# A Fourier mixing and GELU feed-forward kernel: the order of ScalarE's work in a step, the place of one activation, and the steps that carry output sums and transforms

## The chip, the cores and the metric

The kernel runs on one core of one Trainium2 chip. The metric is the time of one execution on the device in microseconds (us). TensorE is PE in the profile (its weight loads are PEld), VectorE DVE, ScalarE ACT, GpSimd POOL, SyncE SP; SP only issues DMAs here. A measurement of this kernel repeats to about 0.2%.

## The reference

The input x is 8 sequences of 3008 rows of 256 numbers, float32. The first block takes a Fourier transform over the rows and then over the columns and keeps the real part; the second is a feed-forward layer with a GELU in its sigmoid form.

```python
X = np.fft.fft(x, axis=1)
X = np.fft.fft(X, axis=2)
x = X.real.astype(np.float32).reshape(8 * 3008, 256)
h = x @ w_in                                # 256 -> 2048
g = h * (1.0 / (1.0 + np.exp(-1.702 * h)))
out = (g @ w_out).astype(np.float32)        # 2048 -> 256
```

## The kernel before, in words

**Symmetry.** The input is real, so the real part of row k of the two transforms and that of its mirror row are a sum and a difference of the same two parts. The kernel transforms the rows only (`mix1`, `stage2`), folds the column transform into w_in once (`fold_w`), and makes for a block of 256 row numbers two products, P (cosine part) and Q (sine part). P + Q is what row k needs before the GELU, P - Q what the mirror row needs.

**Steps.** The work is a list of 384 steps (line 507): 8 sequences, 3 blocks, 2 halves of 256 (or 226) row numbers, and NP = 8 steps of 256 of the 2048 hidden features. A group is the eight steps of one half; outputs add up in PSUM over a group. The first 8 steps run in another form (`hidden`, `rows`). From step 8 on one step t does this:

- `middle(t)` (line 583): ACT writes a bias into the PSUM bank `x` of the step, two L590, one of two banks in turn (`b0`, `b1`).
- `begin(t)` (line 593): PE adds P to it, four matmuls of 128x64 weights and 256 columns (eight records in the trace). `doubled(t)` (line 599): ACT copies 2P to an SBUF tile g, L602. `begin(t, 1)`: PE adds Q, so that the bank holds P + Q. It must wait for L602.
- `forward(t)` (line 604): ACT applies the GELU to the bank and writes A11 and A12 (L605). `backward(t)` (line 607): VectorE takes 2P - (P + Q) with rows reversed (L563) and so has the argument of the mirror rows, in SBUF. `activate_back(t)` (line 611): ACT applies the GELU to it, A21 (L616) and A22 (L617).
- `sums(t)` (line 621): VectorE makes S3 and S1 (L624, L625), POOL S2 and S4 (L626, L627). `deeper` (line 640) does the like a level further down for a pair of steps: two L648 on VectorE a step.
- With a lag of three steps (`LAG`) PE multiplies by w_out, in two nested levels of a scheme with seven products for a 2x2 block matrix: `product` for the first of the seven (planned at 436 ns) and `small_product` for the others (222 ns a pair). Their list for a step comes from `units`, which joins what step t - 3 gives (`now`) and what the pair before left (`late`). The list is worked off in order by `issue(least)`, which issues while the planned cost stays within `least`.

The order of each engine's instructions is that of the program text; nothing reorders it.

**Order of a normal step, before** (line 1075 on): `begin(t, 1)`, `forward(t)`, `issue(1100)`, `begin(t + 1)`, the rest of the list, `backward(t)`, `activate_back(t)`, `doubled(t + 1)`, one `deeper`, `sums(t)`, `middle(t + 2)`, the output sums of `combine_small`, the other `deeper`. In a normal step A21 goes back into the bank `x` in PSUM (`there` is True); the bank is free for the bias of step t + 2 only after the sums.

**Special steps.** 50 steps carry a transform group: `mix1` (28 times; stage one of the next sequence, from input rows that POOL has folded in `fold1`) or `stage2` (22 times, with a small rotation and four transposes on VectorE, L351 and L370). Both borrow the banks `b0` and `b1`. In a special step the list of the next step is issued too, and A21 stays in SBUF (L616 writes `big`).

**End of a group.** Counted by t modulo 8 of the running step: in step 3 `combine` copies from PSUM by ACT (L776, L778, L779) and `combine_small` adds four times on VectorE (L808); `swap` moves halves between partitions by ACT (L817) in 4, 5 and 5; `combine_last` adds in step 6 (L826 twice, L790) and step 0 (L829); `turn_last` transposes in 1 and 2 (L759) and SP stores (L848).

Of the kernel before, what the change touches and what calls it, by code (L numbers as in the profile page):

```python
# [29 lines left out]
ALU = mybir.AluOpType  # L30
# [82 lines left out]
def kernel(ctx: ExitStack, tc, x, w_in, w_out, tab1, tab2, out):  # L113
# [497 lines left out]
    def activate_back(t, there):  # L611

        n = width(t)
        x = xb.pop(t)
        a21[t] = x[:, 0:n] if there else turned_rows(t, n)
        nc.scalar.activation(a21[t], turned_rows(t, n), ACTF.Gelu_apprx_sigmoid)  # L616
        nc.scalar.activation(right(t, A22, n), right(t, A22, n), ACTF.Gelu_apprx_sigmoid)  # L617

    a21 = {}

    def sums(t):

        n, a = width(t), a21.pop(t)
        nc.vector.tensor_tensor(right(t, S3, n), left(t, n), a, op=ALU.subtract)  # L624
        nc.vector.tensor_tensor(right(t, S1, n), a, right(t, A22, n), op=ALU.add)  # L625
        nc.gpsimd.tensor_tensor(right(t, S2, n), right(t, S1, n), left(t, n), op=ALU.subtract)  # L626
        nc.gpsimd.tensor_tensor(right(t, S4, n), right(t, A12, n), right(t, S2, n), op=ALU.subtract)  # L627
# [164 lines left out]
    def group_end(t):  # L792
        return t >= 0 and deep(t) and steps[t][3] == NP - 1

    def combine_small(t):
# [8 lines left out]
        for out, i0, i1 in ((res(RES, KEPT - RES), res(KEPT + 384, 0), both(2, [384, 2], [1, w])),  # L804
                            (res(KEPT + 128, 128), res(KEPT, 0), both(5, [384, 2], [1, w])),
                            (res(RES + 256 + w), res(KEPT + 256), both(5, [1, w])),
                            (res(RES + 256, w - 256), res(KEPT + 128, 128), both(3, [384, 2], [1, w]))):
            nc.vector.tensor_tensor(out, i0, i1, op=ALU.add)  # L808

    def swap(t, part):  # L810
# [8 lines left out]
    def combine_last(t, part):  # L819

        if not group_end(t):
            return
        n = width(t)
        if part == 0:
            for q in range(2):
                nc.vector.tensor_tensor(oc[:, q + 1, :n], oc[:, q, :n], big[:, RES + 1024 + 256 * q:RES + 1024 + 256 * q + n], op=ALU.add)  # L826
            fifth(free(big[:], RES + 768, [0, 2], [1, n]), n)
        else:
            nc.vector.tensor_tensor(oc[:, 0:3, :n], oc[:, 0:3, :n], free(big[:], RES, [256, 3], [1, n]), op=ALU.add)  # L829
# [154 lines left out]
    for b in range(1, B):  # L984
        t0 = (b - 1) * NBLK * NF
        if b == 1:
            loads, groups = (3, 3, 17, 24), (15, 22, 25, 32)
# [29 lines left out]
    n = len(steps)  # L1017
    pending = []

    def issue(least=None):  # L1020
        spent = 0
        while pending and (least is None or spent + pending[0][0] / 2 <= least):
            cost, fn, *args = pending.pop(0)
            fn(*args)
            spent += cost

    def transform(t):
        fn, args = special[t]
        spare[:] = [f"b{(t + 1) % 2}", f"b{t % 2}"]
        fn(*args)  # L1030
        middle(t + 1)
        while waiting:
            m, ps = waiting.pop()
            mixed(m, 1, ps)

    for t in range(n + LAG + 1):
        if t < NP:
# [36 lines left out]
        else:  # L1074
# [16 lines left out]
            if now:  # L1091
# [81 lines left out]
```

## Time and profile before

| what | us |
|---|---|
| median of 3 runs | 2050.18 |
| lowest and highest run | 2048.13 and 2052.48 |
| the profiled execution | 2047.31 |
| its span, first to last instruction | 2045.3 |
| from the start of L605 in step 24 to that in step 376 (44 groups) | 1817.7 |
| PE busy, PEld busy | 1869.8, 1464.5 |
| DVE, ACT, POOL busy | 1678.5, 1247.1, 1039.2 |

The granted TensorE clock is 0.998 over the span. The profile lists instructions by the line of the kernel's text; a tile name stands for all its buffers, and most of the work lies in one large SBUF tile `big`. In the table of waits a row reads: who waited, for whom, total us, times, longest. In the groups: count, busy us, mean ns of one, idle time of the engine just before them. In the timeline: start, us, engine, line, with the idle time before in brackets. Instructions of one engine overlap by some 0.08 us at their ends, so costs by starts are a little below the durations. Matmul ends are modelled.

### The profile page before, as it was taken

Reading aid. Unit: us, or ns where it says so; the run is one execution under the profiler, and the core shown is the slowest. Engines: PE = TensorE matmul, PEld = TensorE weight load, DVE = VectorE, ACT = ScalarE, POOL = GpSimd, SP = SyncE. Lnnn points to the kernel's source line nnn. Section 1 sums busy time; section 2 is a strip of 40 time slices with the busy share of each in tenths; the row PEclk is TensorE's granted clock in tenths of the full one; section 3 lists DMA queues with packets and bytes.
Section 4 is the critical chain, followed back from the end, with each engine's and each line's share of the span. In section 5 each row is a group of like instructions: output and inputs, shape, how many; then the busy total and the mean of one; then the engine's idle time right before and its main releaser. Section 6 shows DMA issues by size and latency. Waiting matters only on the chain. (4 is left out here: it accounts for less than half of the span.)

```text
span 2045.3 us, 61513 instructions
## 1 busy us (share of the span) xinstructions
PE 1869.8 (91%) x25990; PEld 1464.5 (72%) x25990; DVE 1678.5 (82%) x2629; ACT 1247.1 (61%) x2663; POOL 1039.2 (51%) x1053
## 2 busy tenths in 40 slices
PE   8988899999999999899998999999989999999998
PEld 5566767777677777777777777777767777777776
DVE  7978888888787888878788888888887888788885
ACT  6556556665666556566566666666656566656664
POOL 4756654445555555455554555554545544344342
PEclk9999999999999999999999999999999999999999
DMA  8322211212212122211222013210232012101001
GB/s 292 102 70 56 56 50 35 65 31 55 50 44 57 31 55 61 64 26 31 59 72 55 20 32 69 69 48 20 48 72 50 18 24 50 28 12 28 16 12 32
DMA packets 152407, 105.67 MB, mean 52 GB/s; under 512 B 108733, under 2 KB 133341, under 8 KB 151572
## 3 DMA queue, kind: packets, MB, share of 16 engines
q1 hardware_dynamic: 149300, 99.69, 20.0%
q8 instruction: 205, 3.36, 0.7%
q10 hardware_dynamic: 2832, 2.05, 0.4%
q14 instruction: 70, 0.57, 0.1%
HBM read 64.41 MB, written 48.05 MB: 55 GB/s over the span
## 5 line engine op out<-in xcount | busy, mean ns | idle before, releaser
L626 POOL TENSOR_TENSOR big<-big 128x256 f32<-128x256 f32 (+1 forms) x376 | 457.1, 1216 | 924.4 <-DVE big L625 924.3
L185 PE MATMUL x<-pq,wcs 128*64 128x256 f32 (+1 forms) x6016 | 773.8, 381 | 135.4 <-ACT g L602 126.1
L648 DVE TENSOR_TENSOR big<-big 128x768 f32<-128x768 f32 (+1 forms) x736 | 730.9, 993 | 0.0
L185 PEld LDWEIGHTS x<-pq,wcs 128*64 128x64 f32 x6016 | 388.4, 137 | 322.5 <-ACT g L602 166.0
L563 DVE TENSOR_TENSOR big<-g,x 128x512 f32<-128x512 f32 (+2 forms) x440 | 257.2, 596 | 327.6 <-ACT big L605 324.7
L590 ACT ACTIVATE x<-nb,af 128x256 f32<-128x256 f32 (+1 forms) x752 | 356.0, 473 | 165.0 <-DVE big L625 111.3
L685 PE MATMUL low<-big 128*64 128x128 f32 (+1 forms) x6624 | 425.7, 271 | 3.2 <-DVE big L808 2.9
L685 PEld LDWEIGHTS low<-big 128*64 128x64 f32 x6624 | 372.5, 137 | 47.5 <-issue 10.5
L616 ACT ACTIVATE x<-big 128x256 f32<-128x256 f32 (+1 forms) x326 | 124.9, 383 | 330.3 <-DVE big L563 326.4
L627 POOL TENSOR_TENSOR big<-big 128x256 f32<-128x256 f32 (+1 forms) x376 | 301.0, 801 | 29.5
L605 ACT ACTIVATE big<-x 128x512 f32<-128x512 f32 (+1 forms) x376 | 220.2, 586 | 109.3 <-PE x L185 64.6
L602 ACT ACTIVATE g<-x 128x512 f32<-128x512 f32 (+1 forms) x376 | 216.1, 575 | 64.2 <-PE x L185 64.0
L185 PE MATMUL top<-big,wo 128*64 128x256 f32 (+1 forms) x1536 | 227.3, 376 | 3.2 <-DVE os L759 3.2
L685 PE MATMUL mid<-big,wo 128*64 128x128 f32 (+1 forms) x2944 | 214.6, 271 | 0.0
L685 PEld LDWEIGHTS mid<-big,wo 128*64 128x64 f32 x2944 | 175.0, 137 | 21.9 <-DVE big L808 1.4
L685 PE MATMUL low<-big,wo 128*64 128x128 f32 (+1 forms) x2208 | 158.8, 272 | 4.5 <-DVE big L648 4.5
L685 PE MATMUL mid<-big 128*64 128x128 f32 (+1 forms) x2208 | 155.2, 270 | 0.0
L617 ACT ACTIVATE big<-big 128x256 f32<-128x256 f32 (+1 forms) x376 | 149.3, 397 | 0.0
L685 PEld LDWEIGHTS mid<-big 128*64 128x64 f32 x2208 | 130.6, 137 | 16.5
L685 PEld LDWEIGHTS low<-big,wo 128*64 128x64 f32 x2208 | 126.6, 137 | 18.8 <-DVE big L648 7.8
L185 PEld LDWEIGHTS top<-big,wo 128*64 128x64 f32 x1536 | 107.8, 137 | 42.2 <-DVE os L759 3.6
L624 DVE TENSOR_TENSOR big<-big,x 128x256 f32<-128x256 f32 (+1 forms) x326 | 132.4, 406 | 3.9 <-ACT x L616 3.9
(103 smaller groups left out, 1782.9 us busy)
## 6 DMA issues: line engine op xcount, KB each, us to landing
out_dram<-os SPq DMA_DIRECT2D x284, 64.0 KB
t<-Td SPq DMA_DIRECT2D x24, 512.0 KB
Td<-big SPq DMA_DIRECT2D x56, 192.0 KB
big<-in_x_dram SPq DMA_DIRECT2D x56, 128.0 KB
big<-Xr SPq DMA_DIRECT2D x56, 128.0 KB
nb<-Nd SPq DMA_DIRECT2D x23, 256.0 KB
out_dram<-os SPq DMA_DIRECT2D x96, 56.0 KB
Xr<-in_x_dram SPq DMA_DIRECT2D x7, 752.0 KB
```

The costliest lines, as they stand in the source:

```text
L185: nc.tensor.matmul(out[c0:c0 + 64], lhsT=lhs[:, c0:c0 + 64], rhs=rhs, skip_group_check=True, **how)
L563: nc.vector.tensor_tensor(free(out, at + m - 1, [by, 2], [RUN, blocks], [-1, m]), *ins, op=op)
L590: nc.scalar.activation(x[:, i * 256:i * 256 + n], nbt[b, blk][:, hh * 256:hh * 256 + n], ACTF.Copy, scale=af1[:, f:f + 1])
L602: nc.scalar.activation(two(g[:], n), two(xb[t][:], n), ACTF.Copy, scale=2.0)
L605: nc.scalar.activation(front(t), two(xb[t][:], width(t)), ACTF.Gelu_apprx_sigmoid)
L616: nc.scalar.activation(a21[t], turned_rows(t, n), ACTF.Gelu_apprx_sigmoid)
L617: nc.scalar.activation(right(t, A22, n), right(t, A22, n), ACTF.Gelu_apprx_sigmoid)
L624: nc.vector.tensor_tensor(right(t, S3, n), left(t, n), a, op=ALU.subtract)
L626: nc.gpsimd.tensor_tensor(right(t, S2, n), right(t, S1, n), left(t, n), op=ALU.subtract)
L627: nc.gpsimd.tensor_tensor(right(t, S4, n), right(t, A12, n), right(t, S2, n), op=ALU.subtract)
L648: nc.vector.tensor_tensor(out, i0, i1, op=how)
L685: nc.tensor.matmul(pot[name][64 * side:64 * side + 64, at:at + w], lhsT=lhs, rhs=rhs, start=first_in, stop=(p == NP - 2), skip_group_check ...
```

## The change

In a normal step the doubled copy of the next step follows `begin(t + 1)`, ahead of `backward` and `activate_back`, and only 436 ns of the list, not 1100, are issued ahead of `begin(t + 1)`. A21 stays in SBUF always; `middle(t + 2)` comes right after `activate_back`; both `deeper` parts come ahead of `sums`. `combine_small` does two of its four adds in step 3 and two in step 4; `combine_last` and the swaps come a step later, and the former is in three parts. Small products of two of the seven places (7 and 4) move from the list of step 1 of a group to that of step 2, and the first product of step 2 to the list of step 1. The transform groups move to steps with t modulo 8 of 2 and 6 (but for some of the first sequences), with changed amounts issued around them; the step ahead of a special one keeps 666 ns of its list for it. Loads and folds follow.

```diff
-        reversed_sum(big[:, at:at + 256], at_right(t, A22) - at, gt.pop(t), xb[t], width(t), ALU.subtract)
+        reversed_sum(big[:, at:at + 256], at_right(t, A22) - at, gt.pop(t), xb.pop(t), width(t), ALU.subtract)
...
-        x = xb.pop(t)
-        a21[t] = x[:, 0:n] if there else turned_rows(t, n)
-        nc.scalar.activation(a21[t], turned_rows(t, n), ACTF.Gelu_apprx_sigmoid)
+        nc.scalar.activation(turned_rows(t, n), turned_rows(t, n), ACTF.Gelu_apprx_sigmoid)
...
-        n, a = width(t), a21.pop(t)
+        n, a = width(t), turned_rows(t, width(t))
...
-        todo += [(436, product, t, *it) for it in plan(t)]
+        if p != 2 or not deep(t):
+            todo += [(436, product, t, *it) for it in plan(t)]
+        if p == 1 and deep(t):
+            now = [(436, product, t + 1, *it) for it in plan(t + 1)]
         if t >= NP and p % 2 and deep(t):
-            now = [(222, small_product, t, k, pr) for k in (1, 2, 4, 7) for pr in range(PAIRS)]
+            now = [(222, small_product, t, k, pr) for k in ((1, 2) if p == 1 else (1, 2, 4, 7)) for pr in range(PAIRS)] + now
         if t > NP and p % 2 == 0 and deep(t - 1):
-            late = [(222, small_product, t - 1, k, pr) for k in ((5, 6, 3) if p else (5, 3, 6)) for pr in range(PAIRS)]
+            late = [(222, small_product, t - 1, k, pr) for k in ((7, 4) if p == 2 else ()) + (5, 6, 3) for pr in range(PAIRS)]
...
-            loads, groups = (t0 - 21, t0 - 13, t0 - 4, t0 + 3), (t0 - 7, t0, t0 + 16, t0 + 32)
-            folds = [t0 + k for k in (-18, -15, -13, -10, -8, -6, -4, -2, 2, 5, 8, 11, 14, 18, 22, 26)]
+            loads, groups = (t0 - 21, t0 - 13, t0 - 4, t0 + 4), (t0 - 6, t0 + 2, t0 + 18, t0 + 26)
+            folds = [t0 + k for k in (-18, -15, -13, -10, -8, -6, -4, -2, 1, 4, 7, 10, 13, 16, 19, 22)]
...
-        for blk, k in enumerate((39, 56, 72)):
+        for blk, k in enumerate((38, 54, 70)):
...
-    def issue(least=None):
+    def issue(least=None, keep=0):
         spent = 0
+        if keep:
+            least = sum(u[0] for u in pending) - keep
...
             m, ps = waiting.pop()
             mixed(m, 1, ps)
+        middle(t + 2)
...
-            swap(t - LAG - 3, 1)
+            swap(t - LAG - 4, 2)
             combine(t - LAG - 1)
...
-                activate_back(t, False)
-                issue(1350)
+                activate_back(t)
+                issue(2000)
                 deeper(t - 2, 0)
                 deeper(t - 3, 2)
+                deeper(t - 2, 1)
+                deeper(t - 3, 3)
                 sums(t)
                 transform(t)
-                deeper(t - 2, 1)
-                deeper(t - 3, 3)
...
-                middle(t + 2)
-                issue(880)
+                issue(1000)
             else:
-                issue(0 if after else 1100)
+                issue(0 if after else 436)
                 if t + 1 < n:
                     begin(t + 1)
+                    doubled(t + 1)
+                swap(t - LAG - 3, 0)
...
-                issue()
-                if after and t + 1 < n:
-                    doubled(t + 1)
+                issue(keep=666 if soon else 0)
                 if t < n:
                     backward(t)
-                    activate_back(t, True)
-                if not after and t + 1 < n:
-                    doubled(t + 1)
+                if t - LAG - 1 != last:
+                    combine_small(t - LAG - 2, 1)
+                if t < n:
+                    activate_back(t)
+                if t + 2 < n and not soon:
+                    middle(t + 2)
                 deeper(t - 2, 0)
                 deeper(t - 3, 2)
+                deeper(t - 2, 1)
+                deeper(t - 3, 3)
                 if t < n:
                     sums(t)
-                if t + 2 < n and not soon:
-                    middle(t + 2)
-                combine_small(t - LAG - 1)
-                pending += held
-                issue()
-                deeper(t - 2, 1)
-                deeper(t - 3, 3)
-            swap(t - LAG - 2, 0)
-            swap(t - LAG - 3, 2)
-            combine_last(t - LAG - 4, 0)
-            combine_last(t - LAG - 6, 1)
+                combine_small(t - LAG - 1, 0)
...
+            swap(t - LAG - 3, 1)
+            combine_last(t - LAG - 5, 0)
+            combine_last(t - LAG - 5, 1)
+            combine_last(t - LAG - 6, 2)
```

More of the change, by code (lines that the diff above doesn't have):

```diff
@@ L608, in backward, with activate_back @@
         at = TMP + t % 2 * 256
-        reversed_sum(big[:, at:at + 256], at_right(t, A22) - at, gt.pop(t), xb[t], width(t), ALU.subtract)
-    def activate_back(t, there):
+        reversed_sum(big[:, at:at + 256], at_right(t, A22) - at, gt.pop(t), xb.pop(t), width(t), ALU.subtract)
+    def activate_back(t):
         n = width(t)
-        x = xb.pop(t)
-        a21[t] = x[:, 0:n] if there else turned_rows(t, n)
-        nc.scalar.activation(a21[t], turned_rows(t, n), ACTF.Gelu_apprx_sigmoid)
+        nc.scalar.activation(turned_rows(t, n), turned_rows(t, n), ACTF.Gelu_apprx_sigmoid)
         nc.scalar.activation(right(t, A22, n), right(t, A22, n), ACTF.Gelu_apprx_sigmoid)
-    a21 = {}
     def sums(t):
-        n, a = width(t), a21.pop(t)
+        n, a = width(t), turned_rows(t, width(t))
         nc.vector.tensor_tensor(right(t, S3, n), left(t, n), a, op=ALU.subtract)
@@ L793, in group_end, with combine_small @@
         return t >= 0 and deep(t) and steps[t][3] == NP - 1
-    def combine_small(t):
+    def combine_small(t, half):
         if not group_end(t):
@@ L806, in combine_small @@
                             (res(RES + 256 + w), res(KEPT + 256), both(5, [1, w])),
-                            (res(RES + 256, w - 256), res(KEPT + 128, 128), both(3, [384, 2], [1, w]))):
+                            (res(RES + 256, w - 256), res(KEPT + 128, 128), both(3, [384, 2], [1, w])))[2 * half:2 * half + 2]:
             nc.vector.tensor_tensor(out, i0, i1, op=ALU.add)
@@ L826, in combine_last @@
                 nc.vector.tensor_tensor(oc[:, q + 1, :n], oc[:, q, :n], big[:, RES + 1024 + 256 * q:RES + 1024 + 256 * q + n], op=ALU.add)
+        elif part == 1:
             fifth(free(big[:], RES + 768, [0, 2], [1, n]), n)
@@ L986 @@
         if b == 1:
-            loads, groups = (3, 3, 17, 24), (15, 22, 25, 32)
+            loads, groups = (3, 3, 17, 24), (15, 22, 26, 32)
             folds = 11, 12, 13, 14, 16, 17, 19, 20, 21, 22, 23, 24, 26, 28, 29, 30
         else:
-            loads, groups = (t0 - 21, t0 - 13, t0 - 4, t0 + 3), (t0 - 7, t0, t0 + 16, t0 + 32)
-            folds = [t0 + k for k in (-18, -15, -13, -10, -8, -6, -4, -2, 2, 5, 8, 11, 14, 18, 22, 26)]
+            loads, groups = (t0 - 21, t0 - 13, t0 - 4, t0 + 4), (t0 - 6, t0 + 2, t0 + 18, t0 + 26)
+            folds = [t0 + k for k in (-18, -15, -13, -10, -8, -6, -4, -2, 1, 4, 7, 10, 13, 16, 19, 22)]
         for k in range(3):
@@ L1108 @@
                 doubled(t + 1)
[L1109 to L1110 removed]
+                issue(1000)
             else:
[L1112 removed]
+                issue(0 if after else 436)
                 if t + 1 < n:
                     begin(t + 1)
+                    doubled(t + 1)
+                swap(t - LAG - 3, 0)
                 held = [pending.pop() for _ in range(5)][::-1] if t - LAG == last else []
[L1116 to L1118 removed]
+                issue(keep=666 if soon else 0)
                 if t < n:
                     backward(t)
[L1121 to L1123 removed]
+                if t - LAG - 1 != last:
[4 more added lines that the diff above has]
+                    middle(t + 2)
                 deeper(t - 2, 0)
                 deeper(t - 3, 2)
+                deeper(t - 2, 1)
+                deeper(t - 3, 3)
                 if t < n:
                     sums(t)
[L1128 to L1138 removed]
+                combine_small(t - LAG - 1, 0)
+                if held:
+                    combine_small(t - LAG - 1, 1)
+                    pending += held
+                    issue()
+            swap(t - LAG - 3, 1)
+            combine_last(t - LAG - 5, 0)
+            combine_last(t - LAG - 5, 1)
+            combine_last(t - LAG - 6, 2)
             turn_last(t - LAG - 7, 0)
```

## The prediction

> **What bounds the kernel now.** Names first: a step is one round of the loop over t; eight steps make a group, numbered here 0 to 7 by t modulo 8. I read the page's busy times first, then the table of waits over all engines.
>
> ```profile
> PE 1869.8 (91%) x25990; PEld 1464.5 (72%) x25990; DVE 1678.5 (82%) x2629; ACT 1247.1 (61%) x2663; POOL 1039.2 (51%) x1053
> ```
>
> ```profile
> POOL big L626 <- DVE big L625: 924.3, 348, 7.3
> ACT x L616 <- DVE big L563: 326.4, 190, 5.6
> DVE big L563 <- ACT big L605: 324.7, 211, 4.9
> PEld x L185 <- ACT g L602: 166.0, 162, 3.6
> PE x L185 <- ACT g L602: 126.1, 132, 3.2
> ACT x L590 <- DVE big L625: 111.3, 259, 1.4
> ...
> PEld x L185 <- ACT x L590: 39.3, 121, 0.8
> ```
>
> PE is the fullest engine, so only what it waits for counts: the doubled copy (L602), 166.0 us seen at the weight loads, 126.1 us at the matmuls, whose modelled ends cover part of each wait. The timeline of one step 4 shows why the copy is late.
>
> ```profile
> 984.98 0.60 ACT L605 ACTIVATE big<-x 128x512 f32<-128x512 f32 x1
> ...
> 985.79 1.03 PE L185 MATMUL x<-pq,wcs 128*64 128x256 f32 x8
> ...
> 986.65 0.83 PE L685 MATMUL mid<-big,wo 128*64 128x128 f32 x12
> ...
> 987.31 1.48 PE L685 MATMUL low<-big 128*64 128x128 f32 x24
> 987.94 0.68 DVE L563 TENSOR_TENSOR big<-g,x 128x512 f32<-128x512 f32 x1
> 988.54 0.95 DVE L648 TENSOR_TENSOR big<-big 128x768 f32<-128x768 f32 x1
> 988.65 0.39 ACT L616 ACTIVATE x<-big 128x256 f32<-128x256 f32 x1 [3.08 <-DVE big L563]
> 988.98 0.40 ACT L617 ACTIVATE big<-big 128x256 f32<-128x256 f32 x1
> 989.28 0.58 ACT L602 ACTIVATE g<-x 128x512 f32<-128x512 f32 x1
> ...
> 989.91 1.08 PE L185 MATMUL x<-pq,wcs 128*64 128x256 f32 x8 [1.12 <-ACT g L602]
> ```
>
> What L602 copies was complete about 986.9 (the eight matmul records from 985.79, 1.14 us as from the matmuls at 983.84 to the activation at 984.98). But in ACT's queue it stood behind L616 and L617, which wait 3.08 us for VectorE's L563, itself late behind four output sums (L808) and an L648. PE then had nothing to issue.
>
> How much is idle? From the start of L605 in step 24 (172.2 us) to that in step 376 (1989.9) are 44 groups: 41.3 us each. PE's own work by starts in these rows: eight records of a 256-wide product 0.86 (985.79 to 986.65), twelve small ones 0.66. A group has 16 such starts of a step (13.8), 8 first products of 0.43 (3.4) and 84 pairs of small products of 0.22 (18.5); 28 mix1 of 1.03 and 23 stage2 of about 1.3 over 47 groups add 1.3. Sum 37.0. So 4.3 us a group is idle, 202 us in 47 groups: 166 of it the doubled copy, 36 the rest.
>
> **Part 1: the copy goes ahead.** The doubled copy of the next step comes right after the forward activation, and the matmuls that it needs stand 0.43 us into the step, not 1.1. In the rows above it would run about 987.0 to 987.6, before PE runs out at 988.8. No instruction is added. Removed: 166 us (at least 126.1). What comes late next, in the order of the new program:
> - After mix1 (now step 2), step 3 issues on PE two starts (1.72), two pairs (0.44) and the first product (0.43). From PE's start: L605 runs 1.14 to 1.74, the three copies L776, L778, L779 add 0.70 (980.33 to 981.63 with L605: 1.30), the doubled copy ends 3.0. The product waits 0.15 for the copies, the next step 0.25. 0.4 x 28 = 11 us.
> - The bias of step 5 (L590, 0.99 for two) follows: 3.0 + 0.7 for L616 and L617 + 1.0 = 4.7; PE wants it at 3.0 + 0.86 + 0.43 = 4.3. 0.4 x 28 = 10 us.
> - After stage2 (step 6), step 7 has 1.72 + 0.66 on PE; its copy is ready at 2.6. 0.2 x 22 = 4 us.
> - Then VectorE is behind: step 7's own work (L563 0.60, two L648 1.74, two sums 0.66 by starts: 3.0) plus L826 twice and L790 (2.6; 2.9 in the trace at 958.97), started 1.8 after PE's step 7, holds L563 of step 0 until 7.4. The bias of step 1 comes at 4.3 (copy to 2.6, plus 0.7 and 1.0), PE wants it at 3.9: 0.4. That of step 2 comes at 9.8 (L563 ends 8.1), PE wants it at 9.1: 0.7. 1.1 x 22 = 24 us.
>
> Together 49 us. The 36 us of other waits I leave as they are: mix1's wait for L563 (4.9 us at its matmuls) goes, but its second bank and the stage2 bias after the transposes will wait as often. Idle after: 49 + 36 = 85 us, 117 less than 202. By these rows not under 126 - 49 = 77 less, nor over 166 less.
>
> **Part 2: A21 within SBUF.** L616 writes SBUF, and so L590 no longer waits for the sums (111.3 us of ACT, 39.3 of PE at most): it needs only L563, which L616 has waited for already. L616 itself goes from 0.387 to 0.417 us, on an ACT 61% busy: 0.03 x 326 = 10 us if all of it lay on the path, which part 1's 0.7 already contains. The price is VectorE's. Both sums now read SBUF alone; in special steps they already did:
>
> ```profile
> L625 DVE TENSOR_TENSOR big<-x,big 128x256 f32<-128x256 f32 x270 | 111.9, 415 | 0.0
> L624 DVE TENSOR_TENSOR big<-big,x 128x256 f32<-128x256 f32 x270 | 111.1, 411 | 2.4 <-ACT x L616 2.4
> ...
> L625 DVE TENSOR_TENSOR big<-big 128x256 f32<-128x256 f32 x42 | 26.0, 618 | 0.0
> L624 DVE TENSOR_TENSOR big<-big 128x256 f32<-128x256 f32 x42 | 21.6, 515 | 0.0
> ```
>
> The means hide two populations. In the step at 966 us L624 takes 0.95 us, with POOL's L627 ending inside it; L625 just behind it, undisturbed, takes 0.41, as with an input in PSUM. So VectorE loses 0.54 us when POOL got in first. In before, L648 lost 37 us over 608 (1012 against about 951 undisturbed, 0.95 in the timeline) and these sums 13: 1.1 us a group.
>
> [...]
>
> My count for after: L626 now starts right at the end of the sums, because both L648 pairs are moved ahead of them. Where VectorE runs on without a gap, L563 (input in PSUM) covers L626, the first L648 loses about 0.1, and L627 gets in ahead of the second: 0.54. That is steps 5 and 1 (0.65, 0.5) and a little in 2: 1.3 us a group. Where other work lies between (the L808s in 3 and 4, transposes in 6) there is no conflict. Of 16 folds per 48 steps 11 land where VectorE has no gap, at 0 to 1.4 us each, 0.7 in the middle: 1.3 a group. Sum 2.6; the nearest row is 1.1; I take 2.0. Bounds: 0, and 1.3 + 2.5 = 3.8. Of what VectorE loses about half reaches PE: it is busy 33 us of a group and free for some 6, but that free time lies in the special steps, where PE has up to 8 us of work, and none in steps 0, 1 and 5. So 2.0 x 0.5 x 47 = 47 us (0 to 90).
>
> **Part 3: sums and products split.** The L808 adds of step 3 (four, 3.1 us) become two in step 3 and two in step 4; L826, L790 go from 6 to 7; ACT's L817 copies (0.83) go from 4, 5, 5 to 5, 5, 6. Same instructions, same durations; the flattening is in part 1. PE's pairs for two of the seven places wait a step so that L808 has read them, and a first product takes their room: 0, since 0.43 and 1.32 us of PE work only change order. If that cover is gone, PE waits for L808 (2.9 us in before, 0.5 at most each): up to 44 x 0.5 = 22 us.
>
> **Part 4: transforms at steps 2 and 6.** 46 of the 50 special steps move, by one to six steps, with their spills; one load and the later folds move by one to four. On SP's queue they pass the stores (L848), which wait 1267.6 us for transposes, idle time of SP. The fills of stage2 are used one or two steps earlier, still about four steps (20 us) after their issue; PE waits for no fill now. I take 0; if every fill came a microsecond late, 22 us.
>
> **The sum.** 2045.3 - 117 + 47 = 1975 span. Around it lie 2.0 us (the profiled execution took 2047.3), and that execution is 2.9 under the median 2050.2 of the runs: **1980 us**.
>
> **Rivals.**
> - A larger gain: VectorE loses no more than now, 1.1 a group: 26 us in place of 47, 1959; with none, 1933. For it: L648's mean is 6% over its undisturbed time, though POOL works beside it. Against: L626 comes earlier. 0.29 for below 1958.
> - The wait moves from the copy to the bias. PE's first matmuls of the next step stand 0.67 us earlier in its queue and so want L590 that much earlier. If four steps of a group wait 0.3 us more, 4 x 0.3 x 47 = 56 us: 2036. For it: 121 waits of PEld for L590 now. Against: L590 comes 0.8 us earlier too, at the end of L617 (989.4) and not of L625 (990.2). 0.14 for 2012 to 2046.
> - Slower: VectorE becomes the bound through the shared reads. If every step loses 0.54 and every fold 0.8, that is 6.5 us a group, 3.25 on PE: 38.8 (37.0 and 85 / 47) + 3.25 = 42.05 against 41.3, +35 us: 2085. It decides from 5.0 us a group, 0.6 a step, on. For it: VectorE's 82% and the split means. Against: four steps of eight have work between that does not conflict. 0.10.
>
> **How the numbers follow.** Forecast (1958 to 2012) 0.43; larger gain 0.29; bias 0.14; slower 0.10; 0.04 within 0.2% of the median (2046 to 2054), about what a measurement of this kernel can tell from no change. Faster by more: 0.43 + 0.29 + 0.14 = 0.86. The range goes from no loss on VectorE (1933) to the end of the bias case (2046) and leaves out about 0.16.
>
> **What would show it.** In the new profile the waits of PE for the doubled copy should fall from 166 to about 20 us (step 3 and step 7 alone); ACT's wait for L625 should be gone; PE's waits for L590 should rise to about 70, at steps 0, 1 and 4. Both sums should have a mean between 0.45 and 0.6, L648 about 1.05. POOL's L626 should fall from 1.24 us to about 0.8. The forecast is wrong if the sums and L648 together lose over 5.0 us a group, or if PE waits at every step for L590.

## The result and the profile after

The changed kernel takes 2042.0 us (median of 7 runs, 2040.9 to 2044.0) against 2048.9 (7 runs): ratio 0.9967, 95% interval 0.9955 to 0.9978. It is faster by 0.3%, where the forecast had 3.4%. The profiled execution took 2042.8 us, its span 2041.0. Busy times on the page of the changed kernel:

```profile
PE 1894.2 (93%) x25990; PEld 1478.7 (72%) x25990; DVE 1776.5 (87%) x2629; ACT 1235.8 (61%) x2663; POOL 971.5 (48%) x1053
```

VectorE works 98 us longer with the same 2629 instructions. Lines moved by a few: L644 is L648 of before, L620 and L621 are the sums L624 and L625, L622 and L623 POOL's L626 and L627, L614 is L616, L681 is L685, L807 is L808. The table of waits over all engines:

```profile
POOL big L622 <- DVE big L621: 945.1, 348, 7.4
ACT big L614 <- DVE big L563: 306.7, 214, 5.8
...
PEld x L185 <- ACT x L590: 109.4, 125, 3.6
ACT x L590 <- DVE pq L370: 68.2, 22, 4.0
...
PEld low L681 <- DVE big L807: 43.8, 45, 1.3
PEld ps L255 <- DVE big L563: 37.2, 27, 4.0
...
PEld x L185 <- ACT g L602: 20.9, 49, 1.1
```

The doubled copy did what was hoped: 20.9 us in place of 166.0. Three other rows stand in its place: the bias L590 (109.4, was 39.3), the output sums L807, and mix1's wait for L563. The last two wait for VectorE. Of the 109.4 us, 35.6 lie in steps 6 with stage2, 37.5 in step 1 and 23.0 in steps 0 and 4. Followed back along ACT's queue to its last wait, 38 go to the transposes L370, 50 to L563, and 21 to ACT's own waits for PE in L602 and L605. The rows of before with these releasers of VectorE:

```profile
ACT x L590 <- DVE pq L370: 39.3, 22, 2.1
...
PEld ps L255 <- DVE big L563: 8.2, 7, 1.3
...
PEld low L685 <- DVE big L808: 7.2, 19, 0.7
```

A step 4 of the changed kernel in the timeline:

```profile
994.80 0.60 ACT L605 ACTIVATE big<-x 128x512 f32<-128x512 f32 x1
...
994.95 1.03 PE L185 MATMUL x<-pq,wcs 128*64 128x256 f32 x8
...
996.09 0.60 ACT L602 ACTIVATE g<-x 128x512 f32<-128x512 f32 x1 [0.70 <-PE x L185]
...
996.89 1.09 PE L681 MATMUL mid<-big,wo 128*64 128x128 f32 x16 [0.47 <-DVE big L807]
...
997.81 0.68 DVE L563 TENSOR_TENSOR big<-g,x 128x512 f32<-128x512 f32 x1
...
998.25 1.03 PE L185 MATMUL x<-pq,wcs 128*64 128x256 f32 x8
...
998.52 0.42 ACT L614 ACTIVATE big<-big 128x256 f32<-128x256 f32 x1 [1.84 <-DVE big L563]
```

L602 now runs while L614 still waits for L563, and the next product at 998.25 waits for nothing. PE waits for L807 instead. The chain that ended last (the work followed back from the last instruction, each step to what released it) is mostly VectorE's:

```profile
DVE 60%; PE 26%; issue 7%; ACT 4%; DMA 2%; DVEq 0%; POOL 0%; ACTq 0%; SPq 0%
```

VectorE's own instructions, and POOL's beside them, in the groups by form:

```profile
L644 DVE TENSOR_TENSOR big<-big 128x768 f32<-128x768 f32 x608 | 664.0, 1112 | 8.2
L623 POOL TENSOR_TENSOR big<-big 128x256 f32<-128x256 f32 x312 | 305.7, 980 | 24.5
L622 POOL TENSOR_TENSOR big<-big 128x256 f32<-128x256 f32 x312 | 257.0, 824 | 854.7 <-DVE big L621 819.6 <-DVE t L351 35.0
L621 DVE TENSOR_TENSOR big<-big 128x256 f32<-128x256 f32 x312 | 159.8, 512 | 0.0
L620 DVE TENSOR_TENSOR big<-big 128x256 f32<-128x256 f32 x312 | 152.4, 489 | 5.4 <-ACT big L614 5.4
```

The sums rose from 0.41 us in a normal step to 0.49 and 0.51, L644 from 1.01 to 1.11. Over all widths L644 and both sums lose 192 us against their undisturbed times (0.95 and 0.41 us at full width, 0.86 and 0.38 in the narrow half): 4.1 us a group, against 58 us and 1.2 before. A step 6 with stage2 shows where that hurts most:

```profile
1006.64 2.44 DVE L644 TENSOR_TENSOR big<-big 128x768 f32<-128x768 f32 x2
...
1006.95 1.32 POOL L623 TENSOR_TENSOR big<-big 128x256 f32<-128x256 f32 x1
...
1009.01 0.41 DVE L620 TENSOR_TENSOR big<-big 128x256 f32<-128x256 f32 x1
...
1009.34 0.41 DVE L621 TENSOR_TENSOR big<-big 128x256 f32<-128x256 f32 x1
...
1009.68 1.43 DVE L370 STREAM_TRANSPOSE pq<-ps 128x256 f32<-128x256 f32 x4
...
1010.54 1.90 ACT L590 ACTIVATE x<-nb,af 128x256 f32<-128x256 f32 x4 [3.06 <-DVE pq L370]
...
1011.58 0.63 PEld L185 LDWEIGHTS x<-pq,wcs 128*64 128x64 f32 x8 [1.67 <-ACT x L590]
```

POOL's L623 waits for the first L644 (1.32 us, where the one at 1010.64, beside the transposes, takes 0.72) and then holds up the second: the two L644 take 2.44 us, where two undisturbed ones take some 1.8. The transposes stand behind two L644 and two sums, the bias behind the transposes, PE behind the bias.

### The profile page after: what moved, and what is told of

It reads as the page before. It is cut to its first block, busy times and chain, and to the rows that moved or that the text cites. A ratio compares the mean times of both kernels' runs of the same rounds, so it can differ in the third digit from the quotient of the medians.

```text
span 2041.0 us, 61564 instructions
## 1 busy us (share of the span) xinstructions
PE 1894.2 (93%) x25990; PEld 1478.7 (72%) x25990; DVE 1776.5 (87%) x2629; ACT 1235.8 (61%) x2663; POOL 971.5 (48%) x1053
## 3 DMA queue, kind: packets, MB, share of 16 engines
q10 hardware_dynamic: 2832, 2.05, 0.4%
## 4 chain that ended last, share of the span: by engine, by line
DVE 60%; PE 26%; issue 7%; ACT 4%; DMA 2%; DVEq 0%; POOL 0%; ACTq 0%; SPq 0%
DVE big L644 23%; PE x L185 9%; DVE big L563 9%; PE low L681 8%; DVE big L807 7%; DVE big L621 6%; DVE big L620 5%; PE mid L681 3%; DVE big L825 3%; DVE big L789 2%; ACT big L605 2%; PE ps L255 2%; DVE os L758 2%; DVE big L829 1%; ACT x L590 1%
## 5 line engine op out<-in xcount | busy, mean ns | idle before, releaser
L644 DVE TENSOR_TENSOR big<-big 128x768 f32<-128x768 f32 (+1 forms) x736 | 795.9, 1101 | 9.7
L622 POOL TENSOR_TENSOR big<-big 128x256 f32<-128x256 f32 (+1 forms) x376 | 305.6, 813 | 980.1 <-DVE big L621 945.1
L185 PEld LDWEIGHTS x<-pq,wcs 128*64 128x64 f32 x6016 | 405.8, 137 | 264.9 <-ACT x L590 109.4
L681 PE MATMUL low<-big 128*64 128x128 f32 (+1 forms) x6624 | 442.4, 277 | 24.6 <-DVE big L807 24.6
L681 PEld LDWEIGHTS low<-big 128*64 128x64 f32 x6624 | 385.3, 140 | 91.3 <-DVE big L807 43.8
L563 DVE TENSOR_TENSOR big<-g,x 128x512 f32<-128x512 f32 (+2 forms) x440 | 253.4, 587 | 212.1 <-ACT big L605 211.8
L590 ACT ACTIVATE x<-nb,af 128x256 f32<-128x256 f32 (+1 forms) x752 | 350.9, 468 | 82.3 <-DVE pq L370 68.2
L623 POOL TENSOR_TENSOR big<-big 128x256 f32<-128x256 f32 (+1 forms) x376 | 367.4, 977 | 29.5
L614 ACT ACTIVATE big<-big 128x256 f32<-128x256 f32 (+1 forms) x376 | 155.8, 414 | 310.2 <-DVE big L563 306.7
L602 ACT ACTIVATE g<-x 128x512 f32<-128x512 f32 (+1 forms) x376 | 222.7, 592 | 198.2 <-PE x L185 196.2
L605 ACT ACTIVATE big<-x 128x512 f32<-128x512 f32 (+1 forms) x376 | 218.5, 581 | 154.0 <-PE x L185 152.1
L681 PE MATMUL mid<-big,wo 128*64 128x128 f32 (+1 forms) x2944 | 190.3, 271 | 7.6 <-DVE big L807 7.6
L621 DVE TENSOR_TENSOR big<-big 128x256 f32<-128x256 f32 (+1 forms) x376 | 194.0, 516 | 0.0
L620 DVE TENSOR_TENSOR big<-big 128x256 f32<-128x256 f32 (+1 forms) x376 | 181.3, 482 | 7.1 <-ACT big L614 7.1
L681 PEld LDWEIGHTS mid<-big,wo 128*64 128x64 f32 x2944 | 163.1, 137 | 11.5 <-DVE big L807 10.6
L681 PE MATMUL low<-big,wo 128*64 128x128 f32 (+1 forms) x2208 | 156.8, 272 | 0.0
L681 PE MATMUL mid<-big 128*64 128x128 f32 (+1 forms) x2208 | 150.8, 271 | 0.0
L615 ACT ACTIVATE big<-big 128x256 f32<-128x256 f32 (+1 forms) x376 | 150.4, 400 | 0.0
L681 PEld LDWEIGHTS low<-big,wo 128*64 128x64 f32 x2208 | 129.2, 137 | 14.2 <-issue 1.0
```

What stands on the lines that cost most here:

```text
L185: nc.tensor.matmul(out[c0:c0 + 64], lhsT=lhs[:, c0:c0 + 64], rhs=rhs, skip_group_check=True, **how)
L563: nc.vector.tensor_tensor(free(out, at + m - 1, [by, 2], [RUN, blocks], [-1, m]), *ins, op=op)
L590: nc.scalar.activation(x[:, i * 256:i * 256 + n], nbt[b, blk][:, hh * 256:hh * 256 + n], ACTF.Copy, scale=af1[:, f:f + 1])
L602: nc.scalar.activation(two(g[:], n), two(xb[t][:], n), ACTF.Copy, scale=2.0)
L605: nc.scalar.activation(front(t), two(xb[t][:], width(t)), ACTF.Gelu_apprx_sigmoid)
L614: nc.scalar.activation(turned_rows(t, n), turned_rows(t, n), ACTF.Gelu_apprx_sigmoid)
```

## The experiments

Theory A, formed from these views: the shared reads (the sums, with two SBUF inputs, take 0.49 and 0.51 us beside GpSimd's reads of SBUF, and not 0.41) make VectorE the bound; GpSimd's reads and the places of VectorE's instructions against them set the time. Theory B: the copy only moved the wait on ACT from one instruction to another, and the transforms' new places cost the rest. Times are medians; before stood at 2047.5 to 2050.6 us beside these runs. Intervals are at 95%.

### Without GpSimd's long reads

In `sums`, changed kernel:

```diff
-        nc.gpsimd.tensor_tensor(right(t, S2, n), right(t, S1, n), left(t, n), op=ALU.subtract)
-        nc.gpsimd.tensor_tensor(right(t, S4, n), right(t, A12, n), right(t, S2, n), op=ALU.subtract)
+        nc.gpsimd.tensor_tensor(right(t, S2, 16), right(t, S1, 16), left(t, 16), op=ALU.subtract)
+        nc.gpsimd.tensor_tensor(right(t, S4, 16), right(t, A12, 16), right(t, S2, 16), op=ALU.subtract)
```

> The changed kernel with GpSimd's two subtractions of a step (S2 and S4) cut to 16 columns; the rest of S2 and S4 is left out. Theory A: only the folds still block VectorE, the L644 mean falls to about 1.0 us, the sums to 0.43, and a group takes 39 to 39.5 us: 1945 to 1965 us. Theory B: PE's waits at steps 2 and 6 stay, 2030 us or more.

Measured: 1921.4 us, ratio 0.9374 [0.9361, 0.9388], below theory A's range. Groups by form of this run:

```profile
L644 DVE TENSOR_TENSOR big<-big 128x768 f32<-128x768 f32 x608 | 594.6, 998 | 17.8 <-DVE big L644 0.9
L621 DVE TENSOR_TENSOR big<-big 128x256 f32<-128x256 f32 x312 | 130.4, 418 | 0.0
```

L621 is back at its undisturbed time. 121 us of the changed kernel hang on two GpSimd subtractions that are on no chain. Is it their reading or their being there? The next run puts two fills in their place, which write 512 columns each and read nothing:

```diff
-        nc.gpsimd.tensor_tensor(right(t, S2, n), right(t, S1, n), left(t, n), op=ALU.subtract)
-        nc.gpsimd.tensor_tensor(right(t, S4, n), right(t, A12, n), right(t, S2, n), op=ALU.subtract)
+        nc.gpsimd.memset(right(t, S1, 512), 0.0)
+        nc.gpsimd.memset(right(t, S4, 512), 0.0)
```

> The changed kernel with GpSimd's two subtractions of a step put in place by two fills with zero of 512 columns each, which read nothing (S1, S2, S4 and A22 hold zeros, so this part of the computation is left out). They wait for the sums as the subtractions did and take about as long. Theory A in its narrow form (it is the reads that exclude each other): L644 and the sums are no more blocked than with GpSimd's instructions cut short, about 1920 to 1940 us. Rival: any work of GpSimd beside VectorE blocks it, 2020 us or more.

Measured: 1918.2 us (one execution), as without the subtractions, the sums at 484 and 419 ns (there 478 and 418), though the fills take POOL 395 us, 525 ns each. So it is the reads. The trace of the changed kernel shows it by the inputs too, at full width, first without an instruction of GpSimd beside them and then with one, in the mean: with two SBUF inputs L620 takes 0.42 and 0.82 us, L621 0.42 and 1.14, L644 0.95 and 1.24; with one input in PSUM L563 takes 0.68 and 0.67, L807 0.95 and 0.95; with a single input, in SBUF, L758 takes 0.70 and 0.70.

### The subtraction S2 on VectorE in four steps of eight

```diff
-        nc.gpsimd.tensor_tensor(right(t, S2, n), right(t, S1, n), left(t, n), op=ALU.subtract)
+        eng = nc.vector if t % 8 in (0, 4, 5, 7) else nc.gpsimd
+        eng.tensor_tensor(right(t, S2, n), right(t, S1, n), left(t, n), op=ALU.subtract)
```

> The changed kernel with S2 made by VectorE, and not GpSimd, in steps 0, 4, 5 and 7, where VectorE runs on without a gap. It costs VectorE 4 x 0.33 us a group and takes away one of GpSimd's two reads there, 0.54 us each. Theory A: 0.2 to 0.3 us saved in each of four steps, 30 to 50 us in all: 1990 to 2015 us. Rival: VectorE's added work counts in full and the one subtraction left on GpSimd collides as often, 2060 us or more.

Measured: 2042.2 us, 0.9960 [0.9946, 0.9974], the changed kernel's own time, between the two ranges. VectorE's losses fall by about a third, but its busy time is 1780.2 against 1776.5 us: what it no longer waits, it now works. This fits VectorE's total, and not its blocking as such, setting the time.

### A21 back in PSUM

The changed kernel with A21 in the bank `x` in normal steps, and so the bias behind the sums:

```diff
...
-                    activate_back(t)
-                if t + 2 < n and not soon:
-                    middle(t + 2)
+                    activate_back(t, True)
...
                     sums(t)
+                if t + 2 < n and not soon:
+                    middle(t + 2)
```

> The changed kernel with A21 back in PSUM in normal steps, and the bias of step t + 2 after the sums. Theory A (VectorE is the bound and loses time to GpSimd at the shared SBUF reads): the two sums lose their 70 us of blocked time (means back to 0.41 us), so about 1985 to 2010 us. Theory B (the transforms at steps 2 and 6 pile up waits on PE): 2040 us or more, since nothing of that changes and the bias waits for the sums again.

Measured: 2220.6 us, 1.0848 [1.0819, 1.0877]. Theory A missed; the number lies in theory B's open range, but not for the transforms that B names. PE's weight loads wait 367.1 us for L590, and ACT 457.0 us for the second sum: with both L648 ahead of the sums the bank comes free far too late. This order needs A21 in SBUF, whatever that costs VectorE.

### The parts put on the kernel before, one by one

The copy alone:

```diff
                     begin(t + 1)
+                    doubled(t + 1)
...
-                if after and t + 1 < n:
-                    doubled(t + 1)
...
-                if not after and t + 1 < n:
-                    doubled(t + 1)
```

> The kernel before with the doubled copy alone moved ahead, right behind the matmuls that it needs. By the first step of my working PE's wait for the copy (166 us at the weight loads) goes and VectorE loses no more than before (1.1 us a group): about 1960 to 1985 us. Rival: PE's wait moves to the bias, which still stands behind the sums: 2030 to 2048 us, with over 120 us of PEld waiting for L590.

Measured: 2065.3 us, 1.0074 [1.0059, 1.0089]: slower, and beyond the rival's range. Its waits:

```profile
ACT g L602 <- PE x L185: 222.4, 284, 5.3
ACT x L590 <- DVE big L625: 174.3, 274, 1.3
...
PEld x L185 <- ACT x L590: 104.6, 217, 3.5
```

L602 now stands ahead of L616 in ACT's queue: there ACT waits 222.4 us for PE, L616 and then the sums come later, and the bias, which needs the bank that the sums read, later still (174.3 us for L625). The wait moved from the copy to the bias. A21 in SBUF alone (`activate_back(t, True)` made `False`):

> The kernel before with A21 in SBUF alone: copy, bias, order as before. Theory A: it takes nothing off PE's path, since the copy stays behind VectorE, and adds the blocked time of the sums (some 35 us by L624 and L625 in the kernel with both parts): 2050 to 2075 us. Rival: the bank that comes free early is what pays, below 2035 us.

Measured: 2024.8 us, 0.9887 [0.9873, 0.9902]; A missed. Without the new order the shared reads cost less than the earlier free bank brings: PE's weight loads wait 23.4 us for L590 (39.3 before) and 134.7 for the copy (166.0). Both together, with `middle(t + 2)` right behind the activation:

> The kernel before with two parts of the change: the doubled copy ahead, and A21 in SBUF with the bias right behind the activation. Order of the L648s, output sums, products and transforms as before. If it is the SBUF part that makes the early copy pay (the copy alone took 2065), this lies below 2065, at 2030 to 2050, since the sums are now blocked by GpSimd's L627, which falls just there in this order. Rival: the flattened output sums are what pays, then 2055 us or more.

Measured: 2008.8 us, 0.9803 [0.9788, 0.9817], under the range that was expected. One part alone costs 16 us, the other brings 24, both with the bias moved up bring 40; the place of the bias was not tried alone. On this kernel three more single edits. 436 for 1100:

> The two parts that took 2008.8 us, with 436 and not 1100 planned ns of products ahead of the next step's first matmuls. If the earlier matmuls only move PE's wait to the bias: 2009 to 2030 us. If the earlier copy is needed: below 2000 us.

Measured: 1996.7 us, 0.9744 [0.9724, 0.9764]. The loads, folds and transform steps of the change:

> The two parts that took 2008.8 us, with loads, folds and transform groups at the steps of the change. In the changed kernel itself the steps made no difference (2042 either way), so within 8 us of 2009; if steps 2 and 6 are worse for a kernel that is not held by VectorE throughout, above 2017.

Measured: 1983.4 us, 0.9677 [0.9658, 0.9697], better than both expectations: the steps of the transforms bring 25 us here, where they bring nothing in the changed kernel (below). Both of them:

> The copy ahead, A21 in SBUF with the bias right behind, transforms at the steps of the change (so far 1983.4 us), and 436 planned ns of products ahead of the next step's first matmuls (alone worth 12 us). If the two add up: 1965 to 1977 us. If they take away the same wait: 1980 to 1988 us. It has everything of the change but the split of output sums and products, the place of the second L648, and the amounts issued around transforms.

Measured: 1979.6 us, 0.9675 [0.9658, 0.9693], the fastest complete kernel here, 3% under before and the change; by its ratio it is level with the one just above, so that 436 adds nothing that can be told apart there. The split of output sums, swaps and small products (the diff of `units`, `combine_small`, `swap` and `combine_last` above) on the kernel of 2008.8 us:

> The copy ahead, A21 in SBUF and the bias right behind (the two parts that together took 2008.8 us), and in addition the output sums, swaps and products split over steps as the change has them; transforms, their amounts and the place of the two L648 as before. If flattening VectorE's load is worth something, 1975 to 2000 us; if VectorE is short over the whole of a group and not in step 3 alone, within 8 us of 2009; if the later sums collide more with GpSimd, above 2017.

Measured: 2066.9 us, 1.0087 [1.0066, 1.0107]: the split costs 58 us there. Two of its waits:

```profile
PEld ps L255 <- DVE big L563: 61.3, 27, 3.5
...
PEld mid L681 <- ACT big L778: 48.4, 46, 1.2
```

VectorE is late at the transforms (39.4 us in the first row without the split), and PE waits for copies out of PSUM. The third expectation's number came, but not its reason: VectorE loses about 2 us a group to GpSimd with and without the split. The granted clock is half for 75 us of the 44 groups, 14 without the split (0.977 and 0.992 over the span).

### The parts taken from the changed kernel

The transform steps, loads and folds of before:

> The changed kernel with loads, folds and transform groups at the steps of the kernel before. Theory B: PE's 2.4 us of gaps in a group at the special steps go back to those of before, 1990 to 2010 us. Theory A: VectorE has the same work and the same blocked time, within 10 us of 2042.

Measured: 2041.9 us, 0.9963 [0.9948, 0.9978]: no difference. The second L644 pair of a normal step behind the sums:

```diff
                 deeper(t - 2, 0)
                 deeper(t - 3, 2)
-                deeper(t - 2, 1)
-                deeper(t - 3, 3)
                 if t < n:
                     sums(t)
+                deeper(t - 2, 1)
+                deeper(t - 3, 3)
```

> The changed kernel with the second L644 of a step put behind the sums again. Theory C (the order, both L644 ahead of the sums, exposes VectorE): the 90 us that L644 loses to L623 go, and the time falls to 1960 to 1980 us. Theory A (there are too few instructions of VectorE in a step that leave the reads free, whatever the order): the sums lose to L623 what L644 lost, within 15 us of 2042.

Measured: 2023.3 us, 0.9868 [0.9851, 0.9886], between the two: the losses on VectorE fall from 4.1 to 3.0 us a group. The split undone alone:

> The changed kernel with the split alone undone: all four L808 adds in step 3, swaps, last adds and the products of places 7 and 4 as before. If the split costs in the changed kernel too, as it did beside the order of before (2067 against 2009): 1990 to 2020 us. If it costs only beside 1100 planned ns of products: 2035 us or more.

Measured: 2017.8 us, 0.9862 [0.9847, 0.9876]. Both of these:

> The changed kernel with the split undone and the second L648 of a normal step behind the sums. If both cost in the changed kernel and for different reasons (19 us for the order): 15 to 25 us under the kernel that has the split alone undone. If they are one cost: within 6 us of it.

Measured: 2009.6 us, 0.9821 [0.9805, 0.9838], 8 us less: again between the two. That left 30 us to the kernel of 1979.6, and what still differs stands around the transforms. So, on top of the last one, the second L644 pair of a special step behind the transform:

```diff
                 deeper(t - 2, 0)
                 deeper(t - 3, 2)
-                deeper(t - 2, 1)
-                deeper(t - 3, 3)
                 sums(t)
                 transform(t)
+                deeper(t - 2, 1)
+                deeper(t - 3, 3)
```

> The changed kernel with the split undone and the second L648 of a normal step behind the sums (2010 us), and now in a special step too: the second L648 pair stands behind the sums and the transform. Theory A (VectorE's order in special steps: each of 22 stage2 steps makes the bias wait for transposes that stand behind the second L648 pair, 68 us of waits against 46 in the fastest kernel so far; the pause also drops the clock): 1985 to 1995, waits of L590 for L370 near 46 us, half-clock time falls by half. Theory B (the amounts of PE's list around a transform): 2005 to 2012.

Measured: 1987.6 us, 0.9699 [0.9683, 0.9715]. Instead of that, the amounts of before (1350 and 880, nothing kept):

> The changed kernel with the split undone and the second L648 of a normal step behind the sums (2010 us), with the amounts of before around a transform: 1350 and 880, and nothing kept in the step ahead. Theory A (order on VectorE): 2003 to 2012, since PE has the same work to issue in all. Theory B (amounts): 1985 to 1995. In between both count.

Measured: 2007.1 us, 0.9800 [0.9784, 0.9815]. Both:

> Both: the order and the amounts of before in special steps. What is then left against the kernel of 1980 us is the place of the bias of the step after next (ahead of the matmuls that follow a transform, or behind the next doubled copy). Both theories: 1978 to 1990; over 1995 would mean that this place counts too.

Measured: 1983.0 us, 0.9677 [0.9663, 0.9691]. The order on VectorE it is. One row of the waits, of the run at 2009.6 us and of that at 1987.6:

```profile
ACT x L590 <- DVE pq L370: 69.2, 22, 3.9
```

```profile
ACT x L590 <- DVE pq L370: 46.2, 22, 2.2
```

22 stage2 steps, 23 us less wait for the transposes, 22 us less time.

## Why the prediction was wrong

The step that failed is the price of nothing for whatever only changed order: the output sums and products split over steps (Part 3), and the second L644 pair moved ahead of the sums and of the transposes, which has no term of its own. Only PE's work was counted there. The runs show 24 us for the split, 22 for the pair in special steps and 8 for that in normal ones; in the traces VectorE reaches the transposes 1 us later by each of the first two, and by the last it loses 1.2 us a group more to GpSimd.

The runs close into an account (differences of medians; each kernel's ratio is known to some 0.15%, 3 us, a difference of two to some 4). From before to the copy and A21 in SBUF: 2048.9 to 2008.8; with 436 and the new transform steps 1979.6. From there to the change: the place of the bias in special steps +3.4 and the amounts +4.6 (each no more than about the error), the second L644 pair ahead of sums and transposes in special steps +22.0, in normal steps +8.2, the split +24.2: 2042.0. The forecast's net for its first two parts, 70 us off, is about what the copy, A21, 436 and the transform steps bring together (69 us). That is luck: it had the copy bring 117 us and A21 cost 47, while the copy alone costs 16 and A21 alone brings 24. The other 62 us were lost in edits that it priced at nothing or not at all.

- **PE's idle time, 202 us with 166 for the copy.** Right as a reading: the wait went.
- **Part 1, 117 us.** The copy's wait fell to 20.9 us as forecast (about 20). PE's weight loads wait 109.4 us for L590, where the sum's terms came to 34 beside the 36 left over, about 70. Two terms failed. The bias of a stage2 step, which "will wait as often", is waited for 35.6 us, 10.1 before; PE's idle time in such a step is 1.6 us, 33 us in the 21 of the 44 groups, where before it was 0.07 in 14 of them and 1.2 in 7. And steps 0, 1 and 4, where most of the 34 was put, came to 60.5. The total of this row does not tell fast from slow, though: it is 126.7 us in the kernel of 1979.6, with 21.6 in stage2 steps. The copy alone is worth less than nothing (2065.3): that is the second rival's mechanism, which A21 in SBUF with the bias right behind it then undoes.
- **Part 2, VectorE's 2.0 us a group.** By itself right: counted the same way, VectorE loses 2.05 us a group with A21 in SBUF alone, 2.1 with the copy, 2.6 in the kernel of 1979.6; the hand count said 2.6. In the changed kernel it is 4.1, in large part because both L644 pairs stand ahead of the sums: with the second pair of a normal step behind them it is 3.0, with the split undone too 2.6. The term that was too small: L623 "gets in ahead of the second: 0.54. That is steps 5 and 1 (0.65, 0.5) and a little in 2". L644 is blocked by L623 for 88.8 us in 44 groups, 2.0 a group instead of the 1.3 that L622 and L623 were given in all; POOL's folds take about 1.7, where they were given 1.3. With the second pair behind the sums L644's share falls to 18.4 and L620 takes 30.5. L622 at 0.82 us and the sums at 0.49 and 0.51 were as foretold, L644 at 1.11 a little over its 1.05. But these signs did not fit the 2.0 beside them: by the undisturbed times, 16 sums at 0.45 to 0.6 and 16 L648 at 1.05 a group lose 2.2 to 4.6.
- **"About half reaches PE."** It was about 0.7: in the 44 groups VectorE's blocked time, over all its instructions with two SBUF inputs, is some 156 us less without GpSimd's long reads, and the time of these groups 110 us less (1695.5 against 1805.7). Some of the 110 is the clock: half clock falls from 34 to 3 us (0.988 and 0.997 over the span), which is at most 15 us of time by the estimate at the end.
- **Part 3, costed at 0.** It costs 24 us here (14 with the second pair behind the sums, 58 on the kernel of 2008.8). "0.43 and 1.32 us of PE work only change order" looked at PE alone. Mean us from one L605 to the next, and the part of it in which no VectorE instruction ran, by the trace:

| step | changed | split undone | 1979.6 us kernel |
|---|---|---|---|
| 0, normal | 5.35, idle 0.10 | 4.71, 0.03 | 4.71, 0.03 |
| 2 with mix1 | 10.05, 2.78 | 8.74, 2.36 | 7.78, 2.78 |
| 4 | 4.69, 0.11 | 6.94, 0.18 | 6.58, 0.19 |
| 5 | 4.87, 0.03 | 3.97, 0.82 | 3.98, 1.01 |
| 6, normal | 4.37, 0.18 | 3.75, 0.46 | 3.69, 0.44 |
| 6 with stage2 | 10.49, 3.74 | 9.54, 1.71 | 8.42, 0.54 |
| 7 | 3.47, 0.44 | 3.91, 0.34 | 4.07, 0.33 |

  The split takes 2.25 us out of step 4 and puts more into steps 0, 2, 5 and 6. VectorE used to catch up in steps 5 and 6; now it reaches step 6 late. Its idle time lies mostly in the special steps, behind its own work of the step, where it can take up nothing: it waits there for the next L605, and with stage2 that waits for PE, the bias and the transposes. In a step 6 with stage2 the last transpose starts 6.46 us after L605 in the changed kernel, 5.51 with the split undone and 4.51 in the third, and the step is longer by about as much. That this lateness is what lengthens the special steps is read from these rows; for the split it was not tried by itself, for the order in special steps it was (22 us).
- **Part 4, costed at 0.** In the changed kernel the steps themselves are worth 0 (2041.9), on the kernel of 2008.8 they bring 25 us. What the part did not price is the order inside a special step: 22 us.
- **The rivals.** The measured 2042.0 lies in the second's span of 2012 to 2046, the wait moving to the bias, but only by its number: the row of L590 is longer still in the kernel that is 62 us faster. The third, VectorE as the bound "from 5.0 us a group", came half true: VectorE carries 60% of the chain at 4.1 us, since its other work had been moved against it too. The first, less loss on VectorE, was wrong.
- **The two signs of being wrong.** Neither came: the sums and L644 lose 4.1 us a group and not over 5.0, and PE does not wait for L590 at every step. They watched the sizes that had a term, and most of the loss lay where there was none.

What stays open is how the split's 24 us divide between VectorE's lateness and the clock (below): undoing it lowers both. The clock may be much of it: with the second pair of a normal step behind the sums the split costs 10.6 us in the 44 groups, and 27 us instead of 7 run at half clock (0.988 and 0.995 over the span), which is up to 10 us of time by the estimate at the end.

## What to carry to other kernels

Moving A21 from PSUM to SBUF freed its bank here (alone it took the weight loads' wait for L590 from 39.3 to 23.4 us), but the sums, then with two SBUF inputs, took 0.49 and 0.51 us and not 0.41 beside GpSimd's reads. Before such a move count how many instructions with two SBUF inputs stand in one row without a gap beside GpSimd's reading time: the order of that row alone took the loss here from 3.0 to 4.1 us a group. The second L644 pair in special steps, moved without a change of work, cost 22 us here on a second engine that was 82% busy: follow that engine's slack step by step up to the next place where somebody waits for it. Put the parts of a bundle on the old kernel one at a time and then together: one part that cost 16 us alone brought 16 beside another, and the bundle hid a version 3% faster.

## What the hardware showed unexpectedly

The granted clock fell to half, 0.51 in the middle one of the stretches below, after PE's weight loads had paused for 1.79 us. Three stretches of the changed kernel; the columns are the stretch, its length, then busy time and instructions of PE, PEld, DVE, ACT and POOL, then the granted clock and two columns on DMA:

```profile
530.00:532.90 2.90, 1.56 (x23) 0.87 (x20) 2.82 (x4) 0.72 (x2) 1.56 (x3) 1.00 0.29 51
532.90:536.40 3.50, 3.50 (x35) 3.50 (x36) 2.25 (x4) 3.01 (x6) 1.70 (x3) 0.51 0.31 52
536.40:540.00 3.60, 3.60 (x46) 2.76 (x44) 0.00 (x0) 1.16 (x3) 1.12 (x2) 1.00 0.52 82
```

The weight loads had paused 1.79 us until 531.64, waiting for L563. The slow stretch began 1.3 us after PE resumed, and lasted 3.41 us. The 13 slow stretches of this trace begin whole multiples of 3.413 us apart. Laid on that grid, in the 44 groups of this trace, and counting pauses of the weight loads of 0.6 us and more: the window that was idle for 2.55 us was followed by a slow one, of the 17 windows at full clock with 1.76 to 1.87 us 8 were, and none with less was. The one slow window that was followed by another was idle for 2.25. In the trace of the kernel before none of 13 windows from 1.6 to 2.0 us was followed by a slow one. What decides stays open.

In the 44 groups the changed kernel runs 34 us at half clock, before 0; without the split it is 7, with the kernel of 1979.6 us 3 (over the span the granted clock was 0.988, 0.998, 0.994 and 0.996). In the slow stretch above 32 small products took 3.63 us, where at full clock 24 took 1.53 (at 1007.97): some 1.6 us more, a little under half of the stretch. So the estimate from these two rows is that at most half of the time at half clock is lost, 17 us of the 34, and that the pauses of 1.76 us and more in a window that were followed by a slow one may have cost more here than their length.
